# Clustered attention with a gated MLP: no constant matmuls in TensorE's early gaps, and another planned order

## The chip, the cores and the metric

One core of one Trainium2 chip. The metric is the device time of one execution in microseconds (us), as the median of several runs. The engines are named as in the profile: PE (TensorE, the matmuls), PEld (its weight loads), DVE (VectorE), ACT (ScalarE), POOL (GpSimd) and SP (SyncE, here only a queue that issues DMAs).

## What is computed

Attention within clusters for 4 batches of 8 heads, 768 positions of 64 channels, and then a gated MLP with a spatial projection over the 768 positions:

```python
q_assign = argmax(q_n @ c_n.T);  k_assign = argmax(k_n @ c_n.T)      # 16 centroids, normalised
scores = where(q_assign == k_assign, scale * q @ k.T, -1e9)
attn = softmax(scores);  x = concat_heads(attn @ v)                  # (4, 768, 512)
h = relu(x @ w_in);  u, v = h[..., :512], h[..., 512:]
v_n = (v - mean(v)) / sqrt(var(v) + 1e-6)
v_s = w_spatial @ v_n + b_spatial
out = (u * v_s) @ w_out
```

## The kernel before

Every fp32 operand is split into a high and a low fp16 part, and products are summed from two or three fp16 matmuls. The attention runs over 16 pairs of heads, numbered n, four to a batch. For a pair:

- `prep(n)` (line 883) loads k and q of the pair (`raw`) and its values (`vraw`), makes the fp16 parts on ACT and on DVE or POOL, copies halves between partitions by DMA, takes the centroid logits on PE (line 925), finds the one-hot clusters on DVE (lines 955 to 959), transposes them by DMA (line 972) and writes them as extra rows of the operand `hq` (line 984). `values_of` (line 758) makes the parts of the values, and sums them with 12 matmuls (lines 783, 784).
- `shifts(n)` (line 998) finds a row maximum: score matmuls on PE (line 1026), each reduced by DVE (line 1033); the result goes through a DMA transpose (line 1080) and a small write of three rows (line 1081, `hq<-sht`) into `hq`. The final scores wait for that write.
- `attend(n)` (line 1163) takes the final scores (lines 1200 and 1202, a pair of matmuls for 512 columns), exponentials on ACT (line 1207), fp16 parts on ACT (line 1222) and POOL (line 1223), and the product with the values (line 1229, 18 matmuls for a tile of keys). A head's result is normalised on DVE (lines 1273 to 1275), split on ACT and POOL, and a DMA transpose (line 1281, `xT<-xhl`) hands the pair to the MLP. Some pairs take a turned form (`turned`, line 1084) whose probabilities are transposed by DMA.

`mlp(b)` (line 1290) needs all four pairs of its batch. It projects x (line 1301, groups of 24 matmuls of 512 columns, two halves: V first, U later), normalises V, applies the spatial matmul (also line 1301), gates, transposes by DMA (line 1388) and multiplies by `w_out`. V00 below is the first V group of batch 0. The weights come early by DMA and are unpacked on DVE (lines 715 to 717, 700).

All of this is recorded as operations with an engine, a cost in us, dependencies and buffers, and a list scheduler in `Plan.run` (line 343) issues them. In its own clock it takes the engine that can start first, and on it, of the operations that are ready by then, the one with the smallest due time. Due times come from `STARTS`, a packed table with one number for each operation (line 333). What counts as ready follows from modelled costs: an operation's end, the handover `lag` between engines (line 300), and for a DMA the numbers of the table `DMA` (lines 337 to 339). Instructions of an engine, and DMAs of a queue, then run in the order in which they were issued.

The constant matmuls come from `keep_warm` (line 656): each multiplies a tile of ones with itself, 512 columns, into a bank that nobody reads.

```python
o = op("PE", 0.2145, run, after=after, at=at, ..., key=FILLER + k, mms=1)
...
if WARM:
    plan.tag = "y"
    keep_warm(WARM, [c_wt])
```

`WARM` lists 145 earliest times, 2.0 to 45.2 us, and `key=FILLER + k` lets the scheduler take one only when no other PE operation is ready by its own clock. `WARM_END = 5` puts five more ahead of the last group of the last batch (line 1381). They are line 660 in the trace, and are called fillers below.

Of the kernel before, what the change touches and what calls it, by code (L numbers as in the profile page):

```python
# [67 lines left out]
LATE_PAD = 0.0  # L68
EARLY_PAD = 0.0
FETCH = (128, 256, 2.6, 0.95)  # L70
PE_PAD = 0.0
# [162 lines left out]
WARM_END = 5  # L234
# [65 lines left out]
def lag(a, b):  # L300
    if a.dma is not None:
        return 0.0
    return SAME[b] if a.eng == b else PAIR.get((a.eng, b), LAG[a.eng]) + (PE_PAD if b == "PE" else 0.0)


class Plan:
# [14 lines left out]
    def op(self, eng, cost, fn, after=(), use=(), new=(), claim=(), key=0.0, at=0.0, dma=None, turn=False, cols=0, alt=None, due=None, port=None, mms=0):  # L321
# [153 lines left out]
def kernel(  # L475
# [191 lines left out]
        plan.tag = ""  # L667
# [622 lines left out]
    def mlp(b):  # L1290
# [85 lines left out]
        def p_tile(t, tr, pos):  # L1376
# [89 lines left out]
```

## Time and profile before

| What | Value |
|---|---|
| median of 3 runs | 646.55 us (646.25 to 649.39) |
| the profiled execution, its own time | 645.87 us |
| its span, first to last instruction | 644.0 us |
| PE busy | 630.6 us (98%) |
| ACT, POOL, DVE busy | 464.4, 441.4, 415.5 us |
| fillers (line 660) | 150, 43.0 us busy |
| granted TensorE clock, mean | 1.0 of full speed |

The span is what the trace covers; some 2 us of the execution's own time lie outside it. The trace's matmuls overlap, so that the busy time of a matmul (0.38 us for 512 columns) is longer than its share of the queue (0.22 us from start to start); the chain of waits gives the latter. Stretches are in us from the span's start.

### The profile page before, as it was taken

Reading aid. Unit: us, or ns where it says so; the run is one execution under the profiler, and the core shown is the slowest. Engines: PE = TensorE matmul, PEld = TensorE weight load, DVE = VectorE, ACT = ScalarE, POOL = GpSimd, SP = SyncE. Lnnn points to the kernel's source line nnn. Section 1 sums busy time; section 2 is a strip of 40 time slices with the busy share of each in tenths; the row PEclk is TensorE's granted clock in tenths of the full one; section 3 lists DMA queues with packets and bytes.
Section 4 is the critical chain, followed back from the end, with each engine's and each line's share of the span. In section 5 each row is a group of like instructions: output and inputs, shape, how many; then the busy total and the mean of one; then the engine's idle time right before and its main releaser. Section 6 shows DMA issues by size and latency. Waiting matters only on the chain.

```text
span 644.0 us, 16978 instructions
## 1 busy us (share of the span) xinstructions
PE 630.6 (98%) x6753; PEld 381.4 (59%) x6753; DVE 415.5 (65%) x856; ACT 464.4 (72%) x842; POOL 441.4 (69%) x377
## 2 busy tenths in 40 slices
PE   8999999999999999999999999999999989999997
PEld 3567776866676665556555655664556545444443
DVE  5978898997998879656875788767325720231000
ACT  5779997978988996548888888898578873143121
POOL 3478996977998997338889766897689763262110
PEclk9999999999999999999999999999999999999999
DMA  6675788795665754732989798978763499232213
GB/s 185 158 139 125 178 187 188 182 168 131 170 151 123 147 133 106 176 97 58 204 173 187 147 202 142 178 153 152 123 140 58 75 163 183 41 78 71 57 42 99
DMA packets 175173, 88.01 MB, mean 137 GB/s; under 512 B 159315, under 2 KB 162422, under 8 KB 175094
## 3 DMA queue, kind: packets, MB, share of 16 engines
q1 hardware_dynamic: 171350, 80.24, 62.2%
q10 hardware_dynamic: 3744, 6.69, 3.0%
q8 instruction: 53, 0.87, 0.6%
q14 instruction: 26, 0.21, 0.1%
HBM read 27.66 MB, written 6.29 MB: 53 GB/s over the span
## 4 chain that ended last, share of the span: by engine, by line
PE 75%; DVE 6%; ACT 6%; DMA 6%; POOL 3%; issue 2%; SPq 0%; POOLq 0%; ACTq 0%; DVEq 0%
PE acc L1301 35%; PE acc L1229 12%; PE acc L1202 7%; PE acc L1200 6%; PE acc L1026 6%; PE acc L660 3%; ACT p L1137 2%; DMA pt<-pt 2%; DVE nm L1033 2%; POOL pt L1223 2%; DMA gT<-ghl 1%; PE acc L1108 1%; PE acc L1106 1%; DVE lo L909 1%; POOL pt L1147 1%
## 5 line engine op out<-in xcount | busy, mean ns | idle before, releaser
L1223 POOL TENSOR_TENSOR pt<-p,pt 128x768 f16<-128x768 f32 x136 | 229.7, 1707 | 24.1 <-ACT pt L1222 14.0
L1033 DVE TENSOR_REDUCE nm<-acc 128x1 f32<-128x512 f32 (+1 forms) x216 | 139.2, 681 | 21.2 <-PE acc L1026 17.9
L1207 ACT ACTIVATE p<-acc 128x512 f32<-128x512 f32 x216 | 122.5, 601 | 18.4 <-PE acc L1202 12.0
L1301 PE MATMUL acc<-win,xT 128*128 128x512 f16 x576 | 134.3, 379 | 1.5 <-DVE nm L1033 0.8
L1222 ACT CAST pt<-p 128x768 f16<-128x768 f32 x136 | 111.5, 839 | 8.7 <-PE acc L1229 6.6
L1147 POOL TENSOR_TENSOR pt<-p,pt 128x768 f16<-128x768 f32 x48 | 78.8, 1650 | 34.1 <-ACT pt L1146 29.5
L1301 PE MATMUL acc<-vn,wsp 128*128 128x512 f16 x432 | 100.2, 379 | 0.0
L1229 PEld LDWEIGHTS <-pt 128*128 128x128 f16 x2448 | 87.3, 97 | 13.8 <-POOL pt L1223 0.3
L1301 PEld LDWEIGHTS <-xT 128*128 128x128 f16 x576 | 55.1, 98 | 64.2 <-issue 2.5
L1229 PE MATMUL acc<-vhl,pt 128*128 128x65 f16 x2448 | 92.5, 193 | 0.2 <-POOL pt L1223 0.2
L1202 PE MATMUL acc<-hq 81*128 81x512 f16 (+1 forms) x288 | 82.2, 326 | 0.4 <-DMA hq<-sht 0.4
L1200 PE MATMUL acc<-hq,lo 128*128 128x512 f16 (+1 forms) x288 | 82.0, 325 | 0.6 <-ACT p L1207 0.3
L1026 PE MATMUL acc<-hq 80*128 80x256 f16 (+1 forms) x288 | 72.1, 325 | 0.6 <-DVE hq L875 0.4
L1301 PEld LDWEIGHTS <-wsp 128*128 128x128 f16 x432 | 41.4, 98 | 47.3
L1301 PE MATMUL acc<-wou,gT 128*128 128x512 f16 x288 | 68.0, 379 | 0.9 <-DMA gT<-ghl 0.6
L1137 ACT ACTIVATE p<-acc,bi,sl 128x512 f32<-128x512 f32 (+1 forms) x96 | 58.6, 674 | 11.9 <-DVE bi L1129 7.9
L1373 POOL TENSOR_TENSOR ghl<-u,ghl 128x512 f16<-128x512 f32 x24 | 27.9, 1162 | 52.9 <-ACT ghl L1372 52.9
L1371 DVE SCALAR_TENSOR_TENSOR u<-acc,bsp,u 128x512 f32<-128x512 f32 x24 | 17.9, 747 | 66.6 <-PE acc L1301 66.5
L1116 DVE TENSOR_REDUCE nm<-acc 128x1 f32<-128x512 f32 (+1 forms) x72 | 46.3, 682 | 18.5 <-PE acc L1108 18.1
L1146 ACT CAST pt<-p 128x768 f16<-128x768 f32 x48 | 39.8, 838 | 11.9 <-DMA pt<-pt 6.7
L1301 PEld LDWEIGHTS <-gT 128*128 128x128 f16 x288 | 27.5, 98 | 33.1 <-DMA gT<-ghl 1.1
L660 PE MATMUL acc<-ones 128*128 128x512 f16 x150 | 43.0, 396 | 1.6 <-DVE ones L619 1.6
(153 smaller groups left out, 1042.9 us busy)
## 6 DMA issues: line engine op xcount, KB each, us to landing
raw<-in_kqT_dram SPq DMA_DIRECT2D x15, 768.0 KB
vraw<-in_vp_dram SPq DMA_DIRECT2D x16, 384.0 KB
out_dram<-o ACTq DMA_DIRECT2D x24, 256.0 KB
hq<-hq SPq DMA_DIRECT2D x15, 384.0 KB
vn<-in_w_in_dram SPq DMA_DIRECT2D x8, 512.0 KB
hq<-lo SPq DMA_DIRECT2D x15, 192.0 KB
lo<-hq SPq DMA_DIRECT2D x15, 192.0 KB
wraw<-in_wsT_dram SPq DMA_DIRECT2D x12, 192.0 KB
```

Of the source, the lines that this page charges most:

```text
L660: T.matmul(out=tok.t, lhsT=ones, rhs=ones.unsqueeze(1).broadcast_to([P, 4, P]), start=True, stop=True)
L1026: T.matmul(out=acc.t[:, c:c + cs.stop - cs.start], lhsT=hq.t[0:R_SH, 1, h, t * P:(t + 1) * P], rhs=hq.t[0:R_SH, 0, h, cs], start=c == 0, s ...
L1033: V.tensor_reduce(out=nm.t[:, t, k:k + 1] if n == 1 else nm.t[:, t:t + n, k], in_=src, axis=AX.X, op=ALU.max, negate=True)
L1137: A.activation(out=p32[j].t[:, halves[x]], in_=sc.t[:, j * (S - 512):(j + 1) * (S - 512)] if x else sc.t, func=AF.Exp, bias=bi.t[:, t:t + ...
L1147: c = op("POOL", 1.64, lambda pt=pt, j=j, p32=p32: G_.tensor_tensor(out=pt.t[:, S:], in0=p32[j].t, in1=pt.t[:, 0:S], op=ALU.subtract), aft ...
L1200: T.matmul(out=o, lhsT=lo.t[:, h, ks], rhs=hq.t[:, 2, h, cs], start=x == 0, stop=False, skip_group_check=True)
L1202: T.matmul(out=o, lhsT=hq.t[0:R_E, 0, h, ks], rhs=hq.t[0:R_E, 1, h, cs], start=False, stop=True, skip_group_check=True)
L1207: o = op("ACT", 0.6, lambda: A.activation(out=p32[j0].t[:, cs] if n_ == 1 else p32s[:, 2 * p32[0].i:2 * p32[0].i + 2, cs], in_=sc.t if n_ ...
L1222: o = op("DVE" if fast else "ACT", C_CAST if fast else 0.83, lambda pt=pt, p32t=p32t, fast=fast: (V.tensor_copy if fast else A.copy)(out=p ...
L1223: o = op("POOL", 1.64, lambda pt=pt, p32t=p32t: G_.tensor_tensor(out=pt.t[:, S:], in0=p32t(), in1=pt.t[:, 0:S], op=ALU.subtract), after=[o ...
L1229: T.matmul(out=a[:, c * W:c * W + w], lhsT=lhsT, rhs=rhs, skip_group_check=True, **f)
L1301: T.matmul(out=acc.t[:, 0:w], lhsT=lr[m][0], rhs=lr[m][1], start=(m == 0), stop=(m == n - 1))
```

## The change

`WARM` becomes empty and `WARM_END` 0, so that all 150 fillers are gone. `LATE_PAD` adds 0.8 us to the modelled end of every DMA that has a tag (all but the first few), and `PE_PAD` adds 0.15 us to each handover from another engine to PE. `STARTS` is replaced by another table of the same form. The operations, their operands and their dependencies are otherwise the same.

```diff
-LATE_PAD = 0.0
+LATE_PAD = 0.8
 EARLY_PAD = 0.0
 FETCH = (128, 256, 2.6, 0.95)
-PE_PAD = 0.0
+PE_PAD = 0.15
...
 STARTS = (
-    "c-rmR)0Q4k5(VJnQ|DCu-5uK<+crA3ZQJhH=-9Sxt7F@??PPK{m-7Ns-&*^o9-!7<#hGD}#bwD@6xM(xWaZg(){&KDf+?n%WxzZ`Ml8Uhvgj-(i@{>C9{=}0oaH|`6IP(eFJg=0qME2J8jH3fhv+2wi?L$8I3(7I"
...
+    "c-jruV`Cml5J2JC*`4(pwP};owr$(CZQHhO+qP}nw(WcW!+AcOIFJT71Rw+~w1w1A2bMxF$PEktLIFX50SN>e6hwf7aPV-0ePo1DSQx7y$F!IpvtuQ!f#t9h_P_zS8aLofJb;JsI^M=RI27ODcSIhONAb8kH!sRd"
...
-WARM = (2.0, 2.3, 2.6, 2.9, 3.2, 3.5, 3.8, 4.1, 4.4, 4.7, 5.0, 5.3, 5.6, 5.9, 6.2, 6.5, 6.8, 7.1, 7.4, 7.7, 8.0, 8.3, 8.6, 8.9, 9.2, 9.5, 9.8, 10.1, 10.4, 10.7, 11.0, 11.3, 11.6, 11.9, 12.2, 12.5, 12.8, 13.1, 13.4, 13.7, 14.0, 14.3, 14.6, 14.9, 15.2, 15.5, 15.8, 16.1, 16.4, 16.7, 17.0, 17.3, 17.6, 17.9, 18.2, 18.5, 18.8, 19.1, 19.4, 19.7, 20.0, 20.3, 20.6, 20.9, 21.2, 21.5, 21.8, 22.1, 22.4, 22.7
...
-WARM_END = 5
+WARM = ()
+WARM_END = 0
```

The first place is PE's queue at V00, the first MLP group of batch 0 (`acc<-win,xT`). Before, two fillers stand ahead of it, behind a product with the values of pair 4 (`acc<-vhl,pt`):

```order
L1229 MATMUL acc1_114<-vhl0_84,pt3_108 128x64
L1229 LDWEIGHTS pt3_108
L1229 MATMUL acc1_114<-vhl0_84,pt3_108 128x65
L660 LDWEIGHTS ones_76
L660 MATMUL acc0_113<-ones_76 128x512
L660 LDWEIGHTS ones_76
L660 MATMUL acc0_113<-ones_76 128x512
L1301 LDWEIGHTS xT0_99
L1301 MATMUL acc5_118<-win_98,xT0_99 128x512
```

Now it follows on final scores of pair 4, second head:

```order
L1200 MATMUL acc5_118<-hq_895,lo_928 128x512
L1202 LDWEIGHTS hq_895
L1202 MATMUL acc5_118<-hq_895 128x512
L1200 LDWEIGHTS lo_928
L1200 MATMUL acc6_119<-hq_895,lo_928 128x256
...
L1202 MATMUL acc6_119<-hq_895 128x256
L1301 LDWEIGHTS xT0_99
L1301 MATMUL acc3_116<-win_98,xT0_99 128x512
```

Nothing but fillers that stood ahead of V00 stands behind it now, and these operations have moved ahead of it: nine pairs of final scores (lines 1200 and 1202) and two products with the values (line 1229) of pair 4, four score matmuls for the maximum of pair 5 (line 1026), and the 12 sums of pair 5's values (lines 783, 784).

The second place is DVE's queue where the last head of pair 3 is normalised (`rc` and `xn`, lines 1273 to 1275), which V00 needs. Before:

```order
L1033 TENSOR_REDUCE nm0_86<-acc7_120 128x1
L1273 TENSOR_SCALAR rc_2421<-acc4_117 128x6
L1033 TENSOR_REDUCE nm0_86<-acc2_115 128x1
L1274 RECIPROCAL rc_2421<-rc_2421 128x6
L1033 TENSOR_REDUCE nm0_86<-acc6_119 128x1
L1275 TENSOR_TENSOR xn_2436<-acc4_117,rc_2421 128x384
```

And now:

```order
L1033 TENSOR_REDUCE nm1_87<-acc0_113 128x1
L715 TENSOR_SCALAR acc5_118<-vn_103 128x512
L1033 TENSOR_REDUCE nm1_87<-acc7_120 128x2
L716 SCALAR_TENSOR_TENSOR acc5_118<-vn_103,acc5_118 128x512
L1273 TENSOR_SCALAR rc_2330<-acc4_117 128x6
...
L717 SCALAR_TENSOR_TENSOR acc5_118<-vn_103,acc5_118 128x512
L1274 RECIPROCAL rc_2330<-rc_2330 128x6
L1033 TENSOR_REDUCE nm1_87<-acc7_120 128x1
L1275 TENSOR_TENSOR xn_2387<-acc4_117,rc_2330 128x384
```

Eight more DVE instructions stand ahead of that last `xn`: seven reductions for the maxima of pair 5 (line 1033) and one pass of weight unpacking (line 715); none that stood ahead has moved behind.

The third place is SP's queue at pair 3's transpose (`xT<-xhl`), the transfer that V00 waits for. Before:

```order
L911 DMA hq_1869<-lo_1874 64x1536
L910 DMA hq_2358<-hq_2358 64x2x1536
L1080 DMA_TRANSPOSE sht_2395<-shx0_81 128x6x128
L1281 DMA_TRANSPOSE xT0_99<-xhl_2349 128x12x128
L1081 DMA hq_984<-sht_2395 3x768
L710 DMA vn_103<-in_w_in_dram 128x1024
L972 DMA_TRANSPOSE oht_2606<-ohx_80 128x6x128
```

And now:

```order
L710 DMA vn_103<-in_w_in_dram 128x1024
L984 DMA hq_1760<-oht_2290 16x768 x2
L1081 DMA hq_895<-sht_2336 3x768
L1281 DMA_TRANSPOSE xT0_99<-xhl_2263 128x12x128
L984 DMA hq_1760<-oht_2290 17x768
```

The transpose has moved behind the last load of `w_in`, the cluster transpose of pair 6 (line 972), two of its row writes (line 984) and the write of pair 4's shift (line 1081); three copies of pairs 5 to 7 that stood ahead of it now come later.

Further up in SP's queue the same kind of shift write (line 1081) has moved behind other transfers: pair 0's second head behind the cluster transpose of pair 2, pair 1's first head behind pair 4's load of `raw` and a copy of `lo`, its second head behind four row writes, and pair 2's two heads behind a weight load and a copy each.

## Rows read from the trace of the kernel before

**Rows 1.** The page, busy time of an engine (share of the span) and instructions.

```profile
PE 630.6 (98%) x6753; PEld 381.4 (59%) x6753; DVE 415.5 (65%) x856; ACT 464.4 (72%) x842; POOL 441.4 (69%) x377
```

**Rows 2.** By stretch, length, busy PE, PEld, DVE, ACT, POOL, granted clock, DMA share, GB/s.

```profile
0.00:62.70 62.70, 58.49 (x621) 36.22 (x622) 49.59 (x127) 46.15 (x89) 36.39 (x45) 1.00 0.67 155
62.70:141.20 78.50, 78.50 (x1168) 59.22 (x1167) 73.95 (x137) 73.25 (x142) 68.01 (x44) 1.00 0.85 178
141.20:197.00 55.80, 55.62 (x696) 36.24 (x695) 51.15 (x86) 48.74 (x94) 49.30 (x41) 1.00 0.64 154
197.00:546.00 349.00, 344.17 (x3827) 207.27 (x3826) 225.89 (x482) 272.27 (x480) 263.50 (x215) 1.00 0.73 142
546.00:644.00 98.00, 93.78 (x451) 42.45 (x447) 14.95 (x29) 24.00 (x42) 24.15 (x35) 1.00 0.26 64
```

**Rows 3.** The same for line 660 alone: PE, PEld.

```profile
0.00:62.70 62.70, 24.46 (x86) 8.66 (x86) 1.00 0.67 155
62.70:141.20 78.50, 10.66 (x38) 3.49 (x38) 1.00 0.85 178
141.20:197.00 55.80, 6.44 (x22) 1.98 (x21) 1.00 0.64 154
```

**Rows 4.** Line 660, matmuls of 0 to 10 us, then of 62.7 to 197 us.

```profile
L660 PE MATMUL acc<-ones x20: 379/517/634, 1.6 to 9.2; 128*128 128x512 f16 x20
...
L660 PE MATMUL acc<-ones x59: 377/379/382, 86.0 to 196.8; 128*128 128x512 f16 x59
```

**Rows 5.** Chain of waits by line, 62.7 to 197 us, and pieces: start, us, what.

```profile
by line: PE acc L1229 27.8%; PE acc L1026 14.2%; PE acc L1202 13.8%; PE acc L1200 13.8%; PE acc L1301 9.7%; PE acc L660 9.0%; POOL pt L1223 4.0%; PE acc L927 1.3%; PE acc L926 1.3%; PE acc L925 1.3%; issue 1.3%; PE acc L783 1.1%; PE acc L78
...
84.73 0.55 PE acc L1229 x18
86.15 0.87 PE acc L660 x4
88.86 0.21 PE acc L1200
89.07 0.22 PE acc L1202
95.83 0.06 PE acc L783
```

**Rows 6.** Waits of PE, whole run: us in total, times, longest us.

```profile
PE acc L1202 <- DMA hq<-sht: 0.4, 1, 0.4
```

**Rows 7.** DVE: the reductions (page), and pair 3's last normalisation (timeline).

```profile
L1033 DVE TENSOR_REDUCE nm<-acc 128x1 f32<-128x512 f32 (+1 forms) x216 | 139.2, 681 | 21.2 <-PE acc L1026 17.9
...
131.27 0.55 DVE L1275 TENSOR_TENSOR xn<-acc,rc 128x384 f32<-128x384 f32 x1
```

**Rows 8.** Timeline of SP's queue around pair 3's transpose, and of PE at V00.

```profile
135.24 1.44 SPq L1281 DMA_TRANSPOSE xT<-xhl  x1
136.77 0.75 SPq L1081 DMA_DIRECT2D hq<-sht  x1
137.58 0.40 SPq L710 DMA_DIRECT2D vn<-in_w_in_dram  x1
138.03 1.25 SPq L972 DMA_TRANSPOSE oht<-ohx  x1
144.49 2.55 SPq L984 DMA_DIRECT2D hq<-oht  x4
...
141.20 2.97 PE L1301 MATMUL acc<-win,xT 128*128 128x512 f16 x13
```

**Rows 9.** Chain of waits, 0 to 62.7 us: two of its pieces.

```profile
17.34 3.15 DVE nm L1033 x6
...
38.81 6.07 DMA hq<-sht
```

**Rows 10.** The end of the run: chain of waits, then PE's timeline.

```profile
633.60 3.99 DMA gT<-ghl
637.64 2.78 PE acc L1301 x12
...
635.78 1.24 PE L660 MATMUL acc<-ones 128*128 128x512 f16 x5
```

More of the change, by code (lines that the diff above doesn't have):

```diff
@@ new lines @@
+    "^6q>9&%&GWHoPAn#wYRid>|jp$MdCp4lgcS$OZfqzsTS5e;h<WWDpreR*_oN5sgJZF;46j>%;_cK;);7Vu?5_A}JXaref5P`cnm(K$~eh?WaHVg1(WF5i*)ABumQpGLOtI3(78Xpe!ou$R@I#+$<-`8gjTCBPYvo"
+    "a)JzkV8{&7AQohVW>5-ZLVk!2VGsi%AqwI{Tu2L<AQ2>ibdVKdLjoudmtifWgiVkT;z3eK4k;iNB!g^_4{}0b$OToQBvgR<P#0#vELaT7Av@%Nyif#+LP011#h^HphH_8^DnT_U3pJoRG=$2~1X@BPXa|j<HFShd"
+    "FdAw>J!k-3pfhxbHqZxpLtp3y6JRjRfq^gvCc%8z3=3d3EP|tu7@9(Q$O0Ll5afXp&>lWR8HmejLTzXPt)K(+gsw0ICc|`?33Fj8OoJ7$1yZw8tU9a4Ho`903j1LX9D)OI1P;OpI0@I`7@UKPa35~NUAPI);R$?)"
@@ new lines @@
+    "XzU)mgjetu9>O<x244Y~XMaGkpWs+13uZA{BumP&vXrbUYtMQ>e;5uEVJyspWw0L3!v@#^7hnpkge9;I*1;Os4aeaQJb+cO9d^QA*awH<3|xi3@DYAP5bMUqvXN{q8_zyKV)hymvLBFurC^f9W7%1BmW=&_^o+C2"
+    "%(B9)9E-u?vn(u(y?_w*1)|s|U@R@m&xloGP1qndgiU0#*&=p=RfGwwIShq<Fan0bD7XRB*+MwR2EhOr3FBZqoP|qp1q=%?&3?ghwv!!U=h+*U0>87rEH;b7lCxAS5lh38una66%fT|SvaA5h$?~wGtTb!J+OmFZ"
+    "Fzd|@vob6<tH^S(cC0dM!|JlWtRCynTC+Z^C7Z&!viWQPd%*6p`|Jw~!HldJE5b^!@~kAQ#Tv2BtSM{7y0Z$b2CL5+vf8X8>%h9Op==DR$vUwXtS9Tm2C@-s99zMLvl(m;yTop>>+C7}$wsrOY!aKtX0pj_AzQ`H"
@@ new lines @@
+    "u#IdhJIxlb^=vWQ%$BlU>;SvQ9<ozx2Rq63v9s(DyU1>`C+rb>#$K{lEDR$sE~dib*a%m{YxW4<!y9-E$lgH}=25Wtcp6T@Ew~0xA%caoY^*V>!y2&WEE*=o<X940<93{n8*v(&#pbYOY&BcMmaq+M6I;o)v%PE`"
+    "+s(GIbL=>~%5F1(8q;7!yv**fE9^PD!0xf%EF8bFU+f=?#2lCxgD?RW#9~+;yWucwio@|Sd(Ymn59~Ah!9KB2jE53qU?Tj=5Df-UVKBzQB$ya8BEy6j9b;i^OokaSGZw`xSO^<p3+#x!aS9&Al$aY+V;;<j1+Wa("
+    "!X{V;8(<$Sf@QG;*2Jn<7n@^O?1BTaF}A^$*c01hKkSR6a1IW^F}MI%;40jWSMUTz@>pyF=4JU<Ay%9@T!RJKH|)WNu~BR-JIIc*{mf!6%!ZjTE565f_#6MC=aN_BHF!0wj+L=K*2a3+3_D{hY>T~cFpk8r*dIsW"
@@ new lines @@
+    "44jQi@e<y`YZ%I>;S$`8Cvh2W!L4`|FXKbpkN5B{e#9>b{26}2xtM~d<C%B^J_sk_M4XD_a5B!qg?J3-;Wj*k({T|l#<jQ(SK=nzi)Zm1?!bMx9?#$rJdGFd0sg{A_!uoeg%|NA=HdnUd3=dC@IJo6xA+w~kHP;S"
+    "@i_c7{=^Tc_zw*5ARf%)@x+|*L|pUOJcK9ZX?RMWpJ(8yc`;s!SK(!OBVM0(;Vbwmev}{QXZSY0n;+w+`B{F0f8y`?Xa0fz;7k}{MRbu^q!GD9QSp@riBzJPC?Mj9yrR6QD_V+HqO+JOmWn;%jJPT?QBKN5rKuS;"
+    "rA{O$FSViC)RQ{UFj_<V=qO#FyY!j9(;JE|<H-y%zbqxo$t*IPEFr5?BT6SL$=b4>>?YgDuClY-Di6v#va7mCUM7+aWm7psE|iPpY*}CRRD;xLwL@K|UsORpmER<&8mg}vs%EO)>VSHv>gh}}qwFXj$`BP(%~sdd"
@@ new lines @@
+    "dzDjH*3<NSUB--*W94+2M5R-i)Iv2-57n!5AyeIqFfYtnxn8c5=~YgZOI_2q^mE<WEH+!rHxtutVR`sl_J_S-fO~K*kBK{ZI?RXpu@qLocGw+v;ZuBq&+!G;=IwZIKABJF2}Nx24+W3Kqw#R=cyykG$LAS&LY|zb"
+    "=Q(%<UWOOuS@~+dlJDYgd4$Nzi|~fLHLuHS@;baT@5+brZhQnE#b@&wd=sC_ckn~}JioxxixMIkPs=m&Y&<*9$qVt~ycI9a%k!SR0I$d^^Xj}Ruf&`1PP{+w$b0ZUydH1CoAai;F>lKU@o~H_AIm55;rt4}#_#j*"
+    "97PA-ix1%=`4~Q$FXK!25x$16=a={dK8w%e^Z69Mh;QcG`E7ofpWwInV!nkh<ooz?et@6k*ZC9vkl*94`A`0h3lS!gh)JR}77-nAG>*sRIFq*)J8_~oh{w_JFdo6n@e+I*-^%y!wR|0~Eb5B|;<&gX9*bAvGJn9Y"
@@ L223 @@
+    "Ki*IF)BJQl%g^)+{2V{uFYya~Pv74!@~iz?KhH1sEBs2o-f#4~{9eDu@ALcpcE8OZ@|*n*f6!0$i~VkY*dOsn{at_DpYrGZRe#O@@IU=hzteB>C;SC}(ckgc{SANHzxE$I3-G`yztx}i=lmsq(?9c1{bT>efAjym"
+    "4A{T{f6U+W_x&UP!hiCg{TKhs{~vH5W*{=~#J}|K{YU@RfA@bp1w_CE!UE9(A%W<D-~O+M00vY*2LgehKyV;55FUsThzLXl{sYyb%9#"
 )
```

72 lines of the change are left out of this document (27 added, 45 removed).

## The prediction

> **What bounds the kernel now.** I read the page first. PE is busy for 98% of the span [rows 1], but that figure contains the fillers, so the question is what they stand in for. The table by stretch, once for all engines and once for line 660 alone, answers it. From 62.7 to 197 us PE has no gap worth naming (78.50 of 78.50 and 55.62 of 55.80 us [rows 2]), and fillers take part in that: 38 up to 141.2 us and 21 after it [rows 3, 4] (22 by the table, one of them ending across the border; 59 in all). Up to 62.7 us there are 86 of them, 24.46 of 58.49 busy us. From 197 us to 546 us there is none, and PE is idle for 4.83 us only (349.00 less 344.17 [rows 2]): from there on PE's own work sets the pace, and whatever is late or early at 197 us is late or early at the end.
>
> The chain of waits then tells a filler that delays from one that fills a gap anyway. From 62.7 to 197 us, 9.0% of the chain is line 660 [rows 5]; 9.0% of 134.3 us is 12.1 us. A piece of four takes 0.87 us, so one holds the queue for 0.218 us, and 59 take 12.8 us: nearly all of them lie on the chain there. Their busy time in rows 3 is longer, as matmuls overlap.
>
> **The fillers up to 62.7 us: nothing gained.** There the chain goes through other engines: six reductions of DVE in a row, a shift write that takes 6.07 us [rows 9]. The 86 fillers cover gaps in which PE waits in any case. What hides their removal is that waiting.
>
> **The fillers from 62.7 us on.** V00 divides them: it starts at 141.20 us [rows 8], the border that I chose for the tables, so that 38 stand ahead of it and 21 behind. Behind it MLP work of batch 0 is always at hand, so the 21 are a plain gain: 21 x 0.218 = 4.6 us. Ahead of it, 38 x 0.218 = 8.3 us come free, but V00 can't simply move up; it needs pair 3. What the new order puts there instead is real work that used to stand behind V00, priced from rows 5: nine pairs of final scores at 0.21 + 0.22 = 0.43 us, 3.9 us; two products with the values at 0.55, 1.1 us; four score matmuls at 0.22, 0.9 us; twelve sums at 0.06, 0.7 us. Together 6.6 us. If V00 starts no later than before, these 6.6 us are gained; 1.7 us of the 8.3 stay as gaps.
>
> Does V00 stay where it is? DVE has eight more instructions ahead of pair 3's last step, at 0.68 us each [rows 7] (I price the one unpacking pass like a reduction of as many columns): 5.4 us. Between 62.7 us and V00 DVE was idle for 78.50 - 73.95 = 4.55 us [rows 2]; pair 3's last step ended at 131.8 us [rows 7]. So pair 3 is between 0.9 us later (all that idle time used up, as PE no longer holds DVE back) and 5.4 us later. PE did not wait at V00 before: the transpose was issued from 135.24 to 136.68 us, and if it took the 3.99 us of the last DMA transpose [rows 10], it had landed by 139.2 us, 2.0 us early (an estimate from these rows). These 2.0 us cover the 0.9. SP's new order I take at nothing here, with its price under the first rival: the queue has nothing late in it if pair 6's clusters are ready, as they had been before. I take V00 as unmoved.
>
> **The clock.** The mean granted clock was 1.0, but the first fillers ran at the lower level: the median of the 20 up to 10 us is 517 ns and the longest 634, against 379 later [rows 4], which is the step from 1.2 to 2.4 GHz. Without fillers PE is sparse up to some 40 us, and its matmuls there may run at the lower level, 634 - 379 = 255 ns more for 512 columns. Nothing in this trace shows PE sparse without fillers, so I bound it. From below: nothing, since DVE, at 0.68 us a reduction, is slower than a score matmul even at 0.43 us from start to start; six reductions in a row on the chain [rows 9] say so. From above: all of PE's own work of that stretch doubled, which is the second rival. The row it is nearest to is the chain's, with DVE in the lead, so only the handovers count: about eight times a matmul of 512 columns stands between two other engines before the pipeline fills. 8 x 0.255 = 2.0 us, added.
>
> The Trainium skill (TensorE: Matmul & The Clock Gate, Part 1) speaks against this change: it says that the low clock is the default state, that activity releases it, and that idle gaps between bursts bring it back. By that rule the whole sparse stretch would run at 1.2 GHz, and the sum would come out as the second rival has it.
>
> **The five fillers at the end.** The last group waits for a transpose that lands at 633.60 + 3.99 = 637.59 us and starts at 637.64 us; the fillers ran from 635.78 us, in that wait [rows 10]: 0 us. If PE's clock fell meanwhile, 12 matmuls would take 12 x 0.218 = 2.6 us more. The wait without them is 1.9 us; waits that long don't occur after the start of this trace, so it isn't shown. I take nothing, as the stretch after 546 us keeps a clock of 1.00 with 4.22 us idle in it [rows 2], and 2.6 us for the range.
>
> **The rest of the order.** After 197 us there are 4.83 us of idle time to win, and 4.22 us after 546 us that are mostly this last wait. The pads make the planner count on later landings, which argues for fewer waits; but a new order can make as many as it removes. I take zero, with 5 us either way for the range.
>
> **The sum**: -6.6 - 4.6 + 2.0 = -9.2 us. Against the profiled execution's 645.87 us that is 636.7 us. That execution lies 0.7 us under the median of 646.55, so as a median I say **637.4 us**, 1.4% less. About 0.5% (3.2 us) is what a measurement of this kernel can tell from no change.
>
> **Rivals.**
>
> *Pair 3 is late, and V00 takes back what the fillers gave.* For it: DVE was busy for 94% of 62.7 to 141.2 us [rows 2] and has more to do ahead of V00. If none of DVE's idle time can be used, pair 3 is 5.4 us late; its transpose also stands behind a weight load (0.40), a cluster transpose (1.25), two row writes (2.55 / 4 each, 1.3) and a shift write (0.75) [rows 8], 3.7 us. Less the 2.0 us of slack, V00 is 7.1 us late and the 6.6 us are gone, and 0.5 more. -4.6 + 0.5 + 2.0 = -2.1, so 644.4 us as a median: no change. Against it: ACT and POOL have room in that stretch (73.25 and 68.01 of 78.50 us).
>
> *PE stays at 1.2 GHz through the first 62.7 us.* PE's own work there is 58.49 - 24.46 = 34.0 us. Doubled, 68.0 us; it no longer fits the stretch and ends 5.3 us late, and with the 2.0 us of handovers 7.3 us. -6.6 - 4.6 + 7.3 = -3.9, so 642.7 us. Against it: once PE is behind it has no gaps, which is what brought the clock up before; most of these 34.0 us come after 36 us, where it is dense by itself.
>
> *Shift writes stuck in SP's queue, slower.* Five of the writes that final scores of pairs 0 to 2 wait for have moved behind other transfers: by their issue times 1.25 us (cluster transpose), a load and a copy taken like the weight load (0.8), four row writes (2.55), and twice a weight load and a copy (0.8 each) [rows 8], 6.2 us in all. If each also lands 2 us later because it shares the DMA engines with what went ahead (6.07 us in rows 9 against 3.99 in rows 10), that is 10 us more. The sum would be -9.2 + 16.2 = +7.0, 653.6 us. It decides from the point where a write is later than its slack; PE waited for such a write once in the whole run, 0.4 us [rows 6], so the slack exists, but its size isn't shown. It would turn the sign only if more than 9.2 of these 16.2 us came through.
>
> *Better than the sum*: all 12.1 us of the chain's fillers gained, no cost of the clock, half of the 4.83 us of idle time: -14.5, 632.1 us.
>
> **How the numbers follow.** The forecast 0.55 (within some 4 us on either side), the better case 0.10, pair 3 late 0.14, the low clock 0.08, the writes 0.13. Faster by over 0.5%: the forecast, the better case and half of the low clock, 0.69, less a margin of 0.03: 0.66. The same: pair 3 late, the other half of the low clock and the margin, some 0.20. Slower: 0.14. The range goes from 631 us, under the better case, to 649 us: both no-change rivals with the 2.6 and the 5 us of unknowns on them. Left out is the stuck queue, and some tail below. The forecast's own range is 633 to 642 us.
>
> **What would show it.** Right: no line 660; PE's first V00 matmul near 141 us with gaps ahead of it of 1 to 2 us between 62.7 us and it; the last PE group near 628 us; from 10 to 30 us matmuls of 512 columns at over 600 ns, and later at 379. Wrong in the first way: a wait of V00 for the DMA `xT<-xhl`. In the second: a granted clock of half well beyond 40 us. In the third: waits of line 1202 or 1200 for `hq<-sht` of over a microsecond in several places. If waits between 197 and 546 us grow beyond 10 us, the new order itself is at fault and none of the above.

## The result, and the profile after

| | before | changed |
|---|---|---|
| median, 11 executions each | 647.70 us (646.25 to 649.51) | 640.38 us (638.05 to 645.37) |
| profiled execution, own time | 645.87 us | 641.15 us |
| span | 644.0 us | 639.4 us |

The ratio is 0.990, with a 95% interval of 0.9882 to 0.9919: 1.0% faster. The forecast was 637.4 us, in a range of 631 to 649. Two edits lie behind this, the fillers and the order; the experiments below take them apart.

The page's first part of the changed kernel answers to [rows 1]:

```profile
PE 612.2 (96%) x6603; PEld 375.5 (59%) x6603; DVE 411.7 (64%) x856; ACT 462.4 (72%) x842; POOL 445.9 (70%) x377
```

The 150 fillers are gone. The table by stretch of the changed kernel, in the same columns, answers to [rows 2]:

```profile
0.00:62.70 62.70, 44.81 (x462) 30.58 (x463) 45.38 (x116) 40.88 (x79) 32.16 (x42) 0.86 0.59 145
62.70:141.20 78.50, 77.22 (x1162) 59.32 (x1162) 74.96 (x143) 73.73 (x142) 66.68 (x44) 1.00 0.84 173
141.20:197.00 55.80, 55.02 (x745) 36.67 (x742) 52.65 (x95) 51.83 (x102) 51.87 (x45) 1.00 0.69 147
197.00:546.00 349.00, 347.07 (x3842) 209.34 (x3839) 224.32 (x478) 273.06 (x483) 272.07 (x215) 1.00 0.76 146
546.00:639.40 93.40, 88.11 (x408) 39.59 (x406) 14.43 (x28) 22.87 (x40) 23.13 (x34) 1.00 0.29 67
```

Two things stand out. The first stretch has fewer matmuls than before even without fillers, 462 against 621 - 86 = 535, and a mean clock of 0.86. (That mean is too high: the trace's clock records begin with the first rise, at 26.2 us here, and the column counts what lies ahead of it as 1.00.) And from 197 to 546 us PE is idle for 349.00 - 347.07 = 1.93 us, against 4.83 before [rows 2]: 2.9 us come from a stretch in which there never was a filler, and for which I had put the order at nothing.

The timelines of PE, DVE and SP of the changed kernel show V00, pair 3's last `xn` and its transpose, for [rows 7, 8]:

```profile
150.62 5.34 PE L1301 MATMUL acc<-win,xT 128*128 128x512 f16 x24
```

```profile
138.73 0.55 DVE L1275 TENSOR_TENSOR xn<-acc,rc 128x384 f32<-128x384 f32 x1
```

```profile
141.57 1.88 SPq L1281 DMA_TRANSPOSE xT<-xhl  x1
```

V00 starts 9.4 us later than before. Yet PE doesn't wait for it: the waits of PE from 62.7 to 197 us are small ones, in four groups:

```profile
PE acc L1229 <- POOL pt L1223: 0.6, 2, 0.3
PE acc L1026 <- DVE nm L1033: 0.3, 1, 0.3
PE acc L1026 <- ACT p L1207: 0.3, 1, 0.3
PE acc L783 <- ACT p L1207: 0.2, 1, 0.2
```

**A measure for all runs.** Fillers, waits and a low clock all take time from PE's own work, so I count them together: up to a point in time, the loss is that time less the sum, over PE's own matmuls started by then, of the median distance from start to start of a matmul of that form in the trace of before. From the traces of the profiled executions, in us (one execution each: e2's own time is 2.8 us over its median, e9's 4.0 us and before's 1.8 us under, so that a difference of one or two us in the last column says little):

| lost up to | 62.7 | 141.2 | 197 | 546 us |
|---|---|---|---|---|
| before | 26.2 | 34.8 | 39.8 | 47.3 |
| changed | 33.2 | 36.1 | 38.6 | 42.5 |
| e1, order of before, no filler | 27.5 | 36.3 | 40.3 | 50.3 |
| e2, order of before, first 86 fillers | 26.2 | 34.0 | 38.7 | 51.0 |
| e5, start of before, then changed order | 28.0 | 34.2 | 36.4 | 41.2 |
| e8, the same with the 86 fillers | 26.2 | 31.7 | 34.1 | 38.4 |
| e10, changed order, 46 fillers | 28.4 | 32.8 | 34.9 | 38.4 |
| e12, old table with the pads | 28.4 | 35.9 | 39.4 | 46.2 |
| e9, new table without the pads | 32.0 | 38.7 | 43.9 | 55.2 |

The changed kernel is 7 us worse than before at 62.7 us, and makes up 12 us by 546 us.

### The profile page after: what moved, and what is told of

Same layout as the page of the kernel before. It is cut to its first block, busy times and chain, and to the rows that moved or that the text cites. A ratio compares the mean times of both kernels' runs of the same rounds, so it can differ in the third digit from the quotient of the medians.

```text
span 639.4 us, 16608 instructions
## 1 busy us (share of the span) xinstructions
PE 612.2 (96%) x6603; PEld 375.5 (59%) x6603; DVE 411.7 (64%) x856; ACT 462.4 (72%) x842; POOL 445.9 (70%) x377
## 4 chain that ended last, share of the span: by engine, by line
PE 69%; ACT 5%; DVE 3%; issue 1%; POOL 1%; DMA 0%; ACTq 0%; POOLq 0%; DVEq 0%
PE acc L1301 41%; PE acc L1229 7%; PE acc L1200 4%; PE acc L1202 4%; PE acc L1026 3%; PE acc L1106 2%; PE acc L1108 2%; PE acc L1156 1%; PE acc L1155 1%; PE acc L1157 1%; ACT p L1137 1%; ACT p L1207 1%; DVE nm L1033 1%; ACT pt L1222 1%; DVE lo L909 1%
## 5 line engine op out<-in xcount | busy, mean ns | idle before, releaser
L1223 POOL TENSOR_TENSOR pt<-p,pt 128x768 f16<-128x768 f32 x136 | 233.3, 1737 | 37.0 <-ACT pt L1222 27.4
L1229 PEld LDWEIGHTS <-pt 128*128 128x128 f16 x2448 | 90.3, 99 | 18.3 <-POOL pt L1223 4.4
L1147 POOL TENSOR_TENSOR pt<-p,pt 128x768 f16<-128x768 f32 x48 | 80.6, 1688 | 28.8 <-ACT pt L1146 21.3
L1229 PE MATMUL acc<-vhl,pt 128*128 128x65 f16 x2448 | 96.8, 195 | 3.2 <-POOL pt L1223 2.8
L1026 PE MATMUL acc<-hq 80*128 80x256 f16 (+1 forms) x288 | 74.7, 350 | 2.9 <-DVE hq L875 1.2
L1200 PEld LDWEIGHTS <-lo 128*128 128x128 f16 x288 | 27.7, 99 | 21.4 <-issue 2.6
```

What stands on the lines that cost most here:

```text
L1026: T.matmul(out=acc.t[:, c:c + cs.stop - cs.start], lhsT=hq.t[0:R_SH, 1, h, t * P:(t + 1) * P], rhs=hq.t[0:R_SH, 0, h, cs], start=c == 0, s ...
L1147: c = op("POOL", 1.64, lambda pt=pt, j=j, p32=p32: G_.tensor_tensor(out=pt.t[:, S:], in0=p32[j].t, in1=pt.t[:, 0:S], op=ALU.subtract), aft ...
L1200: T.matmul(out=o, lhsT=lo.t[:, h, ks], rhs=hq.t[:, 2, h, cs], start=x == 0, stop=False, skip_group_check=True)
L1223: o = op("POOL", 1.64, lambda pt=pt, p32t=p32t: G_.tensor_tensor(out=pt.t[:, S:], in0=p32t(), in1=pt.t[:, 0:S], op=ALU.subtract), after=[o ...
L1229: T.matmul(out=a[:, c * W:c * W + w], lhsT=lhsT, rhs=rhs, skip_group_check=True, **f)
```

## The experiments

To change one thing at a time, the scheduler's loop is replaced by a recorded order (which operation is issued when, and into which bank each PE result goes). Fillers can then be left out or put in without moving anything else:

```diff
-        while done < len(self.ops):
-            best = None
...
+        for q in by:
+            o = self.ops[q]
...
+            for b, n in EXTRA.get(q, ()):
+                for _ in range(n):
+                    self.filler(b)
+            if o.fn is not None and q not in SKIP:
+                o.fn()
```

`SKIP` holds fillers of the old order, `EXTRA` new ones ahead of an operation (line 1417 in the traces). Every ratio is to the kernel before, timed beside it on the same chip.

### What the fillers are worth: e1 and e2

e1 issues the order of before without any of the 150 fillers (`SKIP` = all of them); e2 keeps the first 86 and leaves out the 64 later ones.

> The kernel before in exactly its own order, with none of the 150 fillers issued. Theory (clock and fillers): the 59 fillers after 62.7 us were in PE's way (12.1 us of the chain), and without the 86 early ones the clock falls around 36 to 53 us and costs 8 us, as in the changed kernel: the granted clock is half for 10 us or more after 26 us, and the time is 3 to 5 us under the kernel before. Rival 1 (the order is what gained): the fillers stood in gaps that are there anyway, so the time is that of the kernel before or up to 8 us above it. Rival 2 (the low clock costs nothing, the new order of SP's queue made the changed kernel 8 us late at 64 to 87 us): 10 to 12 us under the kernel before.

> The kernel before in its own order, with the first 86 fillers (up to 62.7 us) issued and the other 64 not. Theory (clock and fillers): the clock stays up and the 59 fillers are out of the way: 9 to 12 us under the kernel before, so faster than the changed kernel by 2 to 5 us. Rival 1 (the order is what gained): within 2 us of the kernel before. Rival 2 (the low clock costs nothing): the same as e1 within 2 us.

e1: 650.82 us, ratio 1.0064 (1.0043 to 1.0084). e2: 647.46 us, ratio 1.001 (0.9986 to 1.0034).

Both came out as rival 1 had them (e1 up to 8 us above the kernel before, e2 within 2 us), not as the theory. So **the 64 late fillers cost nothing that can be measured**, where I had priced 59 of them at 12.8 us of PE's queue, 11.2 of it gained; and the 86 early ones, which I had called free, are worth 0.54%, 3.5 us (give or take 2, by the two intervals). The stretches of e2, to be read beside [rows 2, 3], show why:

```profile
62.70:141.20 78.50, 73.63 (x1133) 56.17 (x1132) 74.09 (x137) 73.37 (x141) 68.10 (x44) 1.00 0.83 178
141.20:197.00 55.80, 53.12 (x688) 35.06 (x686) 52.01 (x86) 48.96 (x94) 49.68 (x41) 1.00 0.76 153
```

Without the 38 fillers ahead of V00, PE is idle for 78.50 - 73.63 = 4.87 us of the stretch in which it had no gap. V00 moves from 141.20 to 140.44 us, by 0.8 us. The waits of e2's PE from 62.7 to 197 us, the five largest, say what stood right behind the fillers:

```profile
PE acc L1229 <- POOL pt L1223: 2.4, 4, 0.8
PE acc L1229 <- ACT p L1207: 1.2, 2, 0.8
PE acc L1200 <- DVE nm L1033: 0.8, 2, 0.6
PE acc L925 <- ACT p L1207: 0.7, 1, 0.7
PE acc L1026 <- ACT p L1207: 0.7, 2, 0.5
```

All listed waits come to 7.1 us there, against 0.2 us before: POOL, ACT and DVE were late themselves. The fillers held the queue for 12.8 us, and the loss up to 197 us fell by 1.1 us only (39.8 to 38.7); the rest isn't in a listed wait. The chain of waits named the fillers [rows 5], since they ended last; it doesn't say how much later than the next.

### Where the low clock acts: e3, e4, and e6 and e10 against them

e3 is the changed order with 94 fillers in PE's waits up to 54 us, e4 with only the 36 of them after 26.2 us. How many go into a wait was counted from the trace of the changed kernel.

> The changed kernel in its own order, with 94 constant matmuls put into the waits of PE that its trace shows up to 54 us (their number by the length of each wait), into banks that nobody uses at that time. Theory (clock and fillers): the clock stays up from 6 us on, the 8 us that the changed kernel is late at 64 us are mostly gone, and 6 to 8 us of them reach the end: 13 to 15 us under the kernel before, 632 to 634 us. Rival 2 (SP's order made it late): the clock is up but the time is that of the changed kernel within 2 us.

> As e3, with only those 36 of the constant matmuls that stand after 26.2 us, where the changed kernel's clock had come up by itself. Theory (clock and fillers): the fall at 36.4 us is what costs, so the clock stays up after 26 us and the time is that of e3 within 2 us. If the first 26 us at the low clock cost as well, it lies 2 to 4 us above e3. Rival 2: the same as the changed kernel within 2 us.

e3: 642.91 us, ratio 0.9921 (0.99 to 0.9943). e4: 642.50 us, 0.9919 (0.9901 to 0.9938). Neither is better than the changed kernel (0.99), and the 632 to 634 us of the theory didn't come. Yet the fall to the low clock from 36.4 us is mostly gone: from 36.4 to 53.5 us the granted clock is 1.00 in e3 and 0.94 in e4. (In e3 it is at half for 3.4 us from 24.9 us; e4, which has no filler ahead of that, rises to the full clock at 28.2 us and falls for 3.4 us at 35.1 us.) I first read this as "the changed order is late by itself, the clock costs nothing". That reading fell with e6, whose PE and SP queues are the changed kernel's up to some 60 us, and the others up to some 50. The clock of the changed kernel, by stretch, and then that of e6:

```profile
26.20:36.40 10.20, 7.16 (x85) 4.55 (x83) 7.03 (x14) 7.91 (x17) 4.49 (x3) 1.00 0.46 112
36.40:53.50 17.10, 15.99 (x132) 11.26 (x129) 10.81 (x21) 9.26 (x17) 10.27 (x8) 0.50 0.74 133
53.50:62.70 9.20, 8.10 (x131) 6.20 (x130) 8.09 (x16) 8.93 (x18) 7.09 (x5) 1.00 0.40 121
```

```profile
26.20:36.00 9.80, 5.95 (x70) 3.61 (x68) 6.04 (x12) 6.87 (x15) 3.52 (x3) 1.00 0.48 116
36.00:41.20 5.20, 4.47 (x68) 3.57 (x66) 2.81 (x5) 4.89 (x11) 4.66 (x4) 0.67 0.62 80
41.20:62.70 21.50, 19.45 (x248) 14.04 (x245) 19.91 (x37) 16.16 (x32) 15.54 (x11) 1.00 0.78 158
```

The changed kernel ran 17.1 us of this at half the full clock (1.2 of 2.4 GHz), e6 3.4 us (a mean of 0.67 over 5.20 us). In that stretch PE is busy for 15.99 of 17.10 us: here it *is* the bound, and DVE starves (10.81 us). By form and line, 36.4 to 53.5 us, first the changed kernel, then e6 (us busy, mean ns):

```profile
L1026 PE MATMUL acc<-hq 80*128 80x512 f16 x9 | 4.8, 630 | 0.0
L1229 PE MATMUL acc<-wou,p 128*128 128x65 f32 x12 | 2.7, 410 | 0.0
```

```profile
L1026 PE MATMUL acc<-hq 80*128 80x512 f16 x12 | 3.7, 378 | 0.0
L1229 PE MATMUL acc<-wou,p 128*128 128x65 f32 x12 | 1.5, 270 | 0.0
```

One and the same place in the queue, the first cluster logits after these score matmuls, starts at these times in the changed kernel, in e6, in e3 and in e10:

```profile
55.42 0.18 PE L925 MATMUL acc<-cmw,hq 128*128 128x32 f16 x1
```

```profile
50.58 0.18 PE L925 MATMUL acc<-cmw,hq 128*128 128x32 f16 x1
```

```profile
54.54 0.18 PE L925 MATMUL acc<-cmw,hq 128*128 128x32 f16 x1
```

```profile
49.87 0.18 PE L925 MATMUL acc<-cmw,hq 128*128 128x32 f16 x1
```

So the longer low stretch costs some 4.8 us there: up to 35 us the changed kernel's PE is 0.6 us ahead of e6's at the same place of the queue. e3 is late in another way: 30 of its fillers stand between 36 and 51 us, 30 x 0.22 = 6.6 us, counted from gaps of a trace in which PE ran at 1.2 GHz; e10, with 4 fillers there, reaches the place 4.7 us earlier. I had made an experiment that takes away one delay and puts in another of the same size.

### Where the order wins: e5, e6, e7 and e11

Four orders without fillers, each with its first part from one kernel and the rest from the other: e5 has before's first 377 operations (all started by 62.7 us), then the changed order; e6 the changed kernel's first 377, then before's; e7 before's first 911 (up to V00), then the changed order; e11 the changed kernel's first 1286 (up to 197 us), then before's. With other neighbours the banks of PE's results were dealt out anew, each time the one that had been free longest; in e7 two operations behind the changeover are exchanged as well. In outline:

```diff
-order = changed_order
+first = before_order[:377]
+order = first + [q for q in changed_order if q not in set(first)]
```

> No constant matmul. The order of the kernel before for its first 377 operations (all that it had started by 62.7 us), then the changed kernel's order for the rest. By the first theory the changed order loses some 6 us up to 62.7 us (of PE's time there 33.2 us went on something other than PE's own work, against 27.5 us with the order of before and no fillers) and wins more later, and the two parts are independent: first score matmul of pair 1's last steps near 55 to 57 us, V00 near 145 us, and 634.5 us in all (632 to 637), 6 us less than the changed kernel. By the rival the early lateness is only work put off, of which PE then has more at hand, so that it closes its later gaps with it: the start of before makes the later gaps come back, and the time stays at 640 to 642 us.

> The reverse: no constant matmul, the changed kernel's order for its first 377 operations (all that it had started by 70 us), then the order of before. By the first theory both losses are had: 650.8 us (the order of before without fillers) and 6 us more for the start, 656 us (654 to 658). By the rival the late start pays itself back, as it does in the changed kernel: 649 to 652 us.

> No constant matmul. The order of the kernel before for its first 911 operations (all that it had started by 141.2 us, V00's start), then the changed kernel's order. By the first theory with the gain spread over the whole run (from V00 to the end the changed kernel loses 7.3 us, the order of before without fillers 14.0 us) the time is 650.8 - 6.7 = 644 us (642 to 646). By a rival the gain comes from the real work that stands ahead of V00 in the changed order, which this kernel undoes: 649 to 651 us. If the order of before has nothing wrong ahead of V00 at all, 640 us.

> No constant matmul. The changed order for its first 1286 operations (all that it had started by 197 us), then the order of before. From 197 to 546 us PE lost 3.9 us in the changed kernel and 10.0 us in the order of before without fillers; at 197 us the two were 38.6 and 40.3 us. If the gain is spread over the whole order, this kernel comes out 6 us over the changed one: 646.5 us (645 to 648). If the gain is made ahead of 197 us, by the real work that stands ahead of V00, and the later difference is only what follows from that, 640 to 642 us.

| | time, us | ratio (95%) |
|---|---|---|
| e5 | 640.37 | 0.9896 (0.9872 to 0.992) |
| e6 | 652.18 | 1.0074 (1.0051 to 1.0097) |
| e7 | 647.95 | 1.0011 (0.9996 to 1.0026) |
| e11 | 653.42 | 1.0098 (1.0073 to 1.0124) |

The totals of e5 and e6 are the rival's (e6 0.2 us over its range), but they show less than that. e5 stands 5.2 us better than the changed kernel at 62.7 us and only 1.3 us better at 546 us (41.2 against 42.5 in the table). e6 wasn't late in the first place: its clock fell for a short time only, and by the same measure it had lost 28.9 us at 62.7 us, where e1 had lost 27.5 and the theory had counted on 6 us more. So e6 doesn't test whether a late start pays itself back. Nor does a better start always run out: e10, below, has the changed order throughout, is 4.8 us better at 62.7 us and still 4.1 us at 546 us. What the runs do show is that the rest decides more: both kernels that end in the order of before are over 650 us.

e7 and e11 hit none of their expected times. Both lose time right behind the changeover, which I put down to the seam, as each half expects other operations to be done. The stretches of e7 and then of e11:

```profile
141.20:160.00 18.80, 15.53 (x99) 8.20 (x96) 11.46 (x22) 10.00 (x20) 7.79 (x6) 0.73 0.47 101
160.00:546.00 386.00, 383.49 (x4366) 234.54 (x4365) 264.00 (x546) 310.98 (x555) 310.51 (x251) 1.00 0.74 144
```

```profile
197.00:220.00 23.00, 18.26 (x218) 11.73 (x216) 16.21 (x26) 19.13 (x39) 19.77 (x13) 1.00 0.55 131
220.00:546.00 326.00, 319.92 (x3525) 191.39 (x3524) 209.88 (x451) 252.32 (x442) 244.91 (x201) 1.00 0.74 142
```

So their totals don't place the gain, but the stretches behind the seams do. The same two stretches of the changed kernel, and then of e1:

```profile
160.00:546.00 386.00, 383.77 (x4346) 234.20 (x4345) 260.99 (x542) 306.88 (x548) 306.80 (x247) 1.00 0.74 145
220.00:546.00 326.00, 324.57 (x3535) 194.22 (x3532) 201.32 (x443) 250.07 (x439) 249.07 (x201) 1.00 0.75 144
```

```profile
160.00:546.00 386.00, 377.31 (x4291) 229.61 (x4292) 264.02 (x538) 308.01 (x550) 302.01 (x244) 1.00 0.73 143
220.00:546.00 326.00, 320.25 (x3529) 191.52 (x3526) 208.86 (x448) 251.72 (x441) 243.41 (x200) 1.00 0.75 142
```

From 160 to 546 us e7 has 2.51 us of idle PE, the changed kernel 2.23, but e1 8.69. From 220 to 546 us e11 has 6.08 us, nearly as e1 (5.75), and the changed kernel 1.43. The changed order loses less wherever it runs, not only at V00. The table of losses agrees: from 62.7 to 197 us the four kernels that have the changed order there lose 5.4 to 8.4 us, the three with the order of before 12.5 to 13.6; from 197 to 546 us it is 3.5 to 4.8 against 7.5 to 12.3.

### Table and pads apart: e9 and e12

e9 is the changed kernel with both pads at 0; e12 the changed kernel with the table of before, its fillers' entries taken out.

```diff
-LATE_PAD = 0.8
+LATE_PAD = 0.0
-PE_PAD = 0.15
+PE_PAD = 0.0
```

> The changed kernel with LATE_PAD and PE_PAD back at 0: no fillers, the new table, the scheduler's old clock. If the pads make the order (operations behind a transfer are taken only when it has really landed), PE's waits for DMA come back, and the time is that of the order of before without fillers, 648 to 653 us. If the new table alone sets the order and the pads only refine it, 640 to 643 us.

> The changed kernel with the table of before (the numbers of the fillers taken out of it): no fillers, LATE_PAD and PE_PAD as changed, old due times. The new table with the old scheduler (e9) took 658 us, where the same table with the pads took 640.4. If the pads are a gain by themselves, because work behind a transfer is put off until it has really landed, 643 to 647 us. If table and pads only work as the pair for which the table was made, the order is as bad as e9's: 653 to 660 us.

e9: 657.96 us, ratio 1.0162 (1.0134 to 1.0191). e12: 645.17 us, ratio 0.9976 (0.996 to 0.9991).

e12 lies in the range for pads that win by themselves: 0.9976 against e1's 1.0064, 0.9%. But a rival stands untested: e12's order was planned anew without fillers, while e1 replays an order that was planned around them, and in the planner each filler takes PE for 0.2145 us. No run has the old table planned anew without fillers and without pads, so what the pads do of the 0.9% isn't shown. The waits fit the pads in part: from 62.7 to 546 us PE waits for DMAs for 2.3 us in e1 and for 0.2 us in e12. The new table without the pads is the worst of all, over both of its expected ranges; that it holds due times made for a clock with pads is my reading, not shown. Its waits are hardly for DMAs (0.3 us), which is what I had expected, but for exponentials that ACT is late with (e9, 62.7 to 546 us, the three longest):

```profile
PE acc L925 <- ACT p L1137: 2.8, 1, 2.8
PE acc L925 <- ACT p L1207: 1.7, 1, 1.7
PE acc L1200 <- ACT p L1207: 1.5, 2, 0.9
```

### The order and a few fillers: e8 and e10

e8 is e5 with the 86 early fillers of before in their old places; e10 the changed order with 46 fillers up to 41 us, most of them before 26 us and fewer than a wait holds.

The key is the operation that they stand ahead of, the pair the bank and the number:

```diff
+EXTRA = {21: [(0, 16)], 144: [(1, 2)], 164: [(2, 1)], 153: [(3, 8)], 187: [(5, 4)],
...
```

> The kernel e5 (order of before for the first 377 operations, then the changed order) with the 86 constant matmuls that the kernel before has among those operations, in their old places in PE's queue; none later. By the theory that the low clock is what still costs (e5's executions at a mean clock of 0.992 took 639.3 us, at 0.984 643.4; with the order of before the same 86 were worth 650.8 - 647.5 = 3.4 us) the first 62.7 us run at the full clock, the mean clock is 0.997 or more, and the time 637 us (636 to 638.5), below both kernels. By the rival that whatever is won before 62.7 us is given back in the later gaps, as e5 gave back 6 us, 640 us (639.5 to 641).

> The changed kernel with 46 constant matmuls in PE's waits up to 41 us, half as many as in e3 and mostly before 26 us, so that they fill part of a wait and hold up nothing. If e3 and e4 (642.9 and 642.5 us, 2 us over the changed kernel) were slower because their constant matmuls stood in the way between 36 and 54 us, this one keeps the clock up without that price: 637.5 to 639 us. If constant matmuls are no use in this order at all, 640 to 641 us. If they hold up work wherever they stand, 642 us.

e8: 637.05 us, ratio 0.986 (0.9834 to 0.9886). e10: 637.07 us, ratio 0.9847 (0.9823 to 0.9871). e8 came out where the low clock is what still costs, e10 0.4 us under the range for fillers that hold up nothing, and **both beat both kernels** by their medians; e10's interval lies wholly below the changed kernel's, e8's just reaches into it. The first stretch of e10 and of e8:

```profile
0.00:62.70 62.70, 53.38 (x556) 32.54 (x556) 48.98 (x122) 43.49 (x84) 34.04 (x43) 0.95 0.61 152
```

```profile
0.00:62.70 62.70, 57.73 (x621) 36.12 (x622) 49.62 (x127) 46.22 (x89) 36.40 (x45) 1.00 0.69 155
```

So the fillers that the change removes were worth keeping at the start: 3.5 us in the order of before (e1, e2), (0.99 - 0.9847) x 647 = 3.4 us in the changed one (e10), (0.9896 - 0.986) x 647 = 2.3 us in e5's (e8), where the two intervals overlap.

## Why the prediction came near in its sum and was wrong in its terms

The sum was -9.2 us, the measured change is 1.0% of 647.7 us, 6.5 us (5.2 to 7.6), or 7.3 by the medians. The median, 640.38 us, lies inside the forecast's own range of 633 to 642 us. That is luck: the gain expected from the late fillers didn't come, and a gain of about the same size came from a term that was put at zero. The terms:

| term | forecast | shown |
|---|---|---|
| fillers up to 62.7 us, with the low clock | 0 + 2.0 us | +3.5 us, give or take 2 (e1 to e2) |
| fillers after 62.7 us | -4.6 - 6.6 us | +0.6 us (-0.9 to +2.2, e2 to before) |
| rest of the order | 0 | (0.99 - 1.0064) x 647 = -10.6 us, give or take 2 (e1 to changed) |

- **"Nearly all of them lie on the chain": the step that failed.** The rows were read rightly, but a place on the chain isn't a price. I did ask what was late next for V00, and not for the other gaps: 21 fillers behind V00 I called "a plain gain", as MLP work is always at hand. In a recorded order it isn't at hand; it stands behind the instruction that waits. e2 gained 1.1 us of loss up to 197 us (39.8 to 38.7), and nothing at the end. The clock has a part in that end: e2's executions that kept it full took 645.7 us, 1.3 us less than the kernel before beside them, and those in which it fell 650.7 (last section).
- **Real work ahead of V00: right as a movement, wrongly booked.** The 6.6 us of scores and products do stand where fillers were. But that is the new order's doing: with the fillers taken out and the order kept, PE waits there. The changed kernel loses 36.1 - 33.2 = 2.9 us from 62.7 us to V00's old place, e1 8.8, and e5, whose start is e1's and whose order there is the changed one, 6.2.
- **V00 "unmoved": wrong by 9.4 us, and without a wait.** By e10, whose V00 starts at 145.86 us, its lateness is 4.8 us of low clock and 4.6 us of order. Rival 1 said that V00 late takes back the gain one for one. It doesn't here, where PE has other work: no wait for `xT<-xhl` appears.
- **The clock: right kind, short by some 1.5 us, and for the wrong reason.** I counted eight handovers, as PE wasn't the bound; between 36.4 and 53.5 us it was. The Trainium skill (TensorE: Matmul & The Clock Gate, Part 1) says that idle gaps between bursts bring the low clock back, and the trace agrees in that it fell to 0.50 at 36.4 us behind 10.2 us in which PE was idle for 3.0 us, the longest wait being 1.36 us for `lo`. What brought it back at 53.5 us isn't shown: PE had been busy for 94% of the 17.1 us until then, at the low clock all the while. Before 26 us it was low too, as I had said it would be: the score matmuls of 512 columns from 8 to 26 us took

```profile
L1026 PE MATMUL acc<-hq 80*128 80x512 f16 x10 | 5.8, 622 | 1.2 <-DVE hq L875 1.2
```

  622 ns in the mean, against 378 later. (The clock column reads 1.00 there, since no clock record lies ahead of the first rise; the level at the start is read from the matmul's own duration.) Rival 2, PE at 1.2 GHz through the whole first stretch, came closer than I had thought: its sign, half the clock well beyond 40 us, is in the trace, and PE was low up to 26.2 us and from 36.4 to 53.5 us, 43.3 of 62.7 us. From 26.2 to 36.4 us and after 53.5 us it ran at the full clock. Against the 7.3 us that it foresaw, the changed kernel has lost 7.0 us more than before at 62.7 us (e10, with the clock up for longer, 2.2); at 141.2 us 1.3 are left. The measured 640.4 us lie between its 642.7 and the forecast's 637.4.
- **The order after 197 us: "I take zero, 5 us either way".** Here sits a little more than half of the order's gain. The changed order loses 3.9 us from 197 to 546 us (38.6 to 42.5), e1 10.0. With the same start (e5 against e1) 4.4 us of the order's gain lie between 62.7 and 197 us and 5.2 between 197 and 546 us. So the premise that whatever is late or early at 197 us is so at the end fell too. I had said that pads argue for fewer waits, and let the other half of the sentence cancel it. e9 says that the table doesn't do it alone; e12 that with pads and a new plan the old table gets about half of it, the share of the pads being open.
- **The stuck queue (rival 3)** fell: no wait of line 1200 or 1202 for `hq<-sht` is among the changed kernel's.
- **The five end fillers: nothing, as said.** Before, the last group waited for `gT` [rows 10]; now it waits for a bank that ACT reads out, which waits for an output DMA. The chain's last pieces and PE's last group in the changed kernel:

```profile
629.42 2.96 DMA out_dram<-o
632.47 0.60 ACT o L1391
633.08 2.78 PE acc L1301 x12
```

```profile
633.08 2.76 PE L1301 MATMUL acc<-wou,gT 128*128 128x512 f16 x12 [1.73 <-ACT o L1391]
```

The 12 matmuls take 2.78 us, as before with fillers ahead of them. They start at 633.08 us, 5 us behind the 628 us of the forecast's signs.

What stays open: why table and pads fit together so much better than either alone, how much of e12's gain over e1 is the pads' and how much the new plan's, and why e5's lead at 62.7 us runs out where e10's doesn't.

## What to carry to other kernels

Before pricing an operation that stands on the chain of waits, ask of each of its places what would end the same wait next; here, where DVE was busy for 94% and ACT for 93% of the stretch, the answer was: right behind it. When a change brings a new order along, cost the order as a term of its own, by what it loses stretch by stretch, for it can outweigh the edit that is named first. And constant matmuls paid here in the start-up waits, 46 of them as well as 86; in gaps further on they paid nothing (e2), and counted from a trace at the low clock they stood in the way (e3).

## What was not expected of the hardware

- From 36 us on, the same PE queue ran at the low clock for 17.1 us in one execution (the changed kernel's) and for 3.4 us in another kernel's (e6), with PE busy for 94% of the longer stretch. The mean clock of the changed kernel's 11 executions went from 0.984 to 0.997: the three at 0.994 or more took 639.3 us in the mean, the five at 0.989 or less 642.3. The four executions of e10, with 46 fillers, lie within 636.95 to 637.50 us, but e8's five, with 86, spread over 3.0 us, so that fillers take the scatter away isn't shown.
- In e2 the clock fell far from the start, towards the end of a single wait for a DMA (247.60 - 240.70 = 6.90 us at 0.51; the wait ends at 241.34 us), in a stretch that ran at 1.00 before. The wait, and the stretches around it:

```profile
PE acc L1026 <- DMA hq<-oht: 2.6, 1, 2.6
```

```profile
197.00:240.70 43.70, 40.91 (x561) 27.36 (x558) 32.68 (x63) 40.37 (x81) 40.86 (x36) 1.00 0.64 114
240.70:247.60 6.90, 6.26 (x36) 3.30 (x37) 3.18 (x5) 3.81 (x7) 5.14 (x4) 0.51 0.63 147
247.60:546.00 298.40, 294.93 (x3172) 174.61 (x3170) 189.73 (x413) 226.55 (x391) 216.88 (x176) 1.00 0.74 143
```

Four of e2's twelve executions had a mean clock of 1.0 and took 645.7 us in the mean; the five at 0.995 or less took 650.7. Only one of the slower ones has a trace. In it the price of a late gap was the gap and the low clock that followed on it; the 5 us between the two groups are more than the 2.6 us of the wait.
